# Cosformer attention into Sinkhorn-routed experts on one core: Sinkhorn's column total by an all-ones product, the second expert's weights in the load buffers, the last block's second layer in quarters, another order for the fourth batch

## The chip, the cores and the metric

The kernel runs on one core of one Trainium2 chip. The metric is device time in microseconds (us). Three runs of the kernel before gave 992.42, 992.71 and 993.43 us; the median is 992.71 us. A profiled execution, whose trace is used below, took 992.42 us, of which the hardware profiler's span is 990.7 us.

## What is computed

A linear attention over 8 batches of 8 heads, 576 positions and 64 features feeds a mixture of 8 experts, in which every token goes through every expert and the results are summed with weights from a Sinkhorn balancing. Cut to what matters:

```python
# attention: q, k, v are [8, 8, 576, 64]
phi(x) = concat(relu(x) * cos(pos), relu(x) * sin(pos))      # 128 features
num = phi(q) @ (phi(k).T @ v);   den = phi(q) @ phi(k).sum(over positions) + 1e-6
x = num / den, as [4608 tokens, 512]
# experts
P = exp(x @ w_gate - max)                                    # [4608, 8]
for _ in range(8):
    P /= P.sum(1) + 1e-9          # rows: each token over the experts
    P /= P.sum(0) + 1e-9          # columns: each expert over the tokens
    P *= 4608 / 8
out = sum over e of P[:, e] * (relu(x @ w1[e]) @ w2[e])      # w1: 512 x 1024, w2: 1024 x 512
```

## The kernel before

Tokens are kept transposed as matmul operands (`xT`, fp16), and results gather in fp32 accumulators (`acc_lo`, and `acc_hi` for the last four groups of 128 tokens). Parts of the accumulators that are not needed yet are lent to the attention: tables, two of the eight transposed-q buffers (`q_pTs`, numbers 6 and 7 in `acc_lo` and `acc_hi`) and the fp16 values.

The first phase mixes attention with the first expert. Block j of 512 tokens goes through that expert (8 `ffn1` slots of 4 matmuls, then 8 `ffn2` slots of 4 matmuls, so 16 slots) while batch j+1 gets its attention, and batch j+2's q, k and v are being loaded. Which step of the attention stands in which slot is written out by hand with `at(block, slot, step)`. The steps of a batch are, for each of its four head pairs hk:

- `load`: six DMAs of 288 KB, issued by POOL (GpSimd), one for each half of q, k and v, into the `ld` pool with four buffers of each. A load with `held_back` waits for the last VectorE (DVE) instruction that was written before it.
- `prep_q`: ReLU and the multiplication with the cosine and sine table on DVE, into one of three `q_p` buffers; from batch 2 on, the result is turned by a transposing DMA, issued by SP. The first of batch 3 also waits until that batch's last load has landed.
- `prep_k` (ReLU of k, on ScalarE, ACT), then `prep_kv`: `prep_kp` (the table's multiplication on DVE) and `prep_v` (a copy of v into its fp16 place).
- `sums`: the products of keys and values of two head pairs, whose results ACT and DVE bring to SBUF (`kv_sb`, `zsel`).
- `denominators`: 24 small matmuls over all transposed q of the batch, then DVE's reciprocal.
- `attend`, one for each hk: matmuls spread the reciprocals (`rb`, copied by ACT) and make the numerators; DVE multiplies the two into `xT`.
- `gates`: logits of a batch's tokens and their exponential.

TensorE, DVE and ACT run in the written order (`te`, `ve` and `se` chain each instruction to the one before it on its engine). SP and POOL are ordered by the framework's scheduler. So an instruction that waits holds all that is written behind it on its engine.

At the end of the first phase its pools are freed and other pools take the memory. The second expert's weights (`wB`, 16 KB in each partition) come first there, so they lie where the first pools of the phase lay: before, `hA` (the first expert's hidden values `hT`, in use until the last ffn2 of block 6), `cs_pool` (small constants) and part of `ld`.

Blocks 7 and 8 of the first expert follow with the Sinkhorn balancing (`sinkhorn`, a generator that yields five times in each of its 8 iterations, and that `balanced` moves on), then the first part of expert 1 with the seven-product method: each `group` calls a fill function seven times, and the first time round `start_fill` puts in a share of block 8's ffn2 and a step of the balancing. Some of those steps carry sums and differences of expert 1's first weights (`w1_steps`), dealt out to iterations by `tw_steps`. The remaining experts follow in a regular stream of products to the end.

In Sinkhorn, P lies as 128 partitions x 36 groups x 8 experts. A column total needs a sum over partitions: before, a matmul with a column of ones gives totals on one partition, DVE takes the reciprocal of these 8 numbers, and a second matmul with a row of the constant N/E spreads them to all partitions, where DVE multiplies.

Of the kernel before, what the change touches and what calls it, by code (L numbers as in the profile page):

```python
# [10 lines left out]
FP32 = mybir.dt.float32  # L11
# [14 lines left out]
def kernel(  # L26
# [154 lines left out]
    with ExitStack() as p1:  # L181
        hA = p1.enter_context(tc.tile_pool(name="hA", bufs=1))
        cs_pool = p1.enter_context(tc.tile_pool(name="cs_pool", bufs=1))
# [5 lines left out]
        rb_pool = p1.enter_context(tc.tile_pool(name="rb_pool", bufs=4))  # L189
        ps_y = p1.enter_context(tc.tile_pool(name="ps_y", bufs=2, space=bass.MemoryType.PSUM))  # L190
# [120 lines left out]
        scale_row = const.tile([1, 2, P], FP32, name="scale_row")  # L311
        ve.memset(scale_row[:, 0, :], float(N) / float(E))
        ve.memset(scale_row[:, 1, :], float(N) / float(E) / XS)
# [338 lines left out]
        for j in range(B):  # L652
            b = j + 1
            if j == 0:
# [4 lines left out]
                for hk in range(HK):  # L659
                    if hk == 3:  # L660
                        at(0, 7, sums_first, 0)
                    for i in range(3):
                        at(0, (5, 6, 6, 7)[hk], turn, 1, hk, i, i != 1)
                    if hk == 0:
                        at(0, 5, prep_q, 1, 3)
                    if hk >= 2:
                        at(0, 4 + hk, prep_v, 1, 2 * hk - 4, se.copy)
                        at(0, 4 + hk, prep_v, 1, 2 * hk - 3, ve.tensor_copy)
                at(0, 7, sums_first, 1)
# [4 lines left out]
            elif b < B:  # L674
# [14 lines left out]
                elif j == 2:  # L689
                    at(j, 0, prep_kv, b, 3)  # L690
                    at(j, 1, sums, b, 0)
                    at(j, 3, sums, b, 1)
                else:
                    at(j, 0, sums, b, 1)
                at(j, 6 if j == 1 else 5 if j == 2 else 3, denominators, b)
                for hk in range(HK):
                    at(j, (9, 10, 12, 13)[hk] if j == 1 else (8 if j == 2 else 6) + 2 * hk, attend, b, hk)
# [558 lines left out]
```

The softmax here doesn't subtract the row's maximum and nothing guards it: scores larger than these inputs give would overflow.

## Time and profile before

| | |
|---|---|
| median of three runs | 992.71 us |
| the profiled execution | 992.42 us |
| its span in the trace | 990.7 us |
| TensorE busy | 969.6 us, 98% |
| VectorE busy | 807.7 us, 82% |
| ScalarE busy | 564.1 us, 57% |
| GpSimd busy | 60.7 us, 6% |
| chain that ended last | TensorE 93%, DMA 2%, VectorE 2%, ScalarE 2% |

The busy share says how full an engine is on the average over the whole span. The list of waits says whom an engine waited for, and how long. A time line gives instructions in order of start, and a window sums them over a stretch. The granted clock is TensorE's share of its full clock. An idle engine costs nothing by itself; only what moves the last engine's end does.

### The profile page before, as it was taken

What the parts mean: (1) busy time and instruction counts of PE and PEld (TensorE: products, weight loads), DVE (VectorE), ACT (ScalarE), POOL (GpSimd) and SP (SyncE); (2) the same over time, 40 slices, a digit from 0 to 9 for tenths busy, and PEclk for the clock granted to TensorE, in tenths of its full rate; (3) what the DMA queues carried; (4) which work ended last, traced back from release to release, by engine and by line L of the source; (5) the groups of instructions that cost most, each with busy time, mean ns of one, the idle gap of its engine ahead of it and who ended that gap; (6) DMA issues with size and microseconds to landing.
All of it is one profiled execution on the core that took longest, in us unless ns stands there. A gap on an engine that the chain in (4) does not pass through costs nothing.

```text
span 990.7 us, 20271 instructions
## 1 busy us (share of the span) xinstructions
PE 969.6 (98%) x7871; PEld 675.4 (68%) x7871; DVE 807.7 (82%) x1835; ACT 564.1 (57%) x1261; POOL 60.7 (6%) x82
## 2 busy tenths in 40 slices
PE   9997999989999999999999999999999999999997
PEld 6443444447777777777777777777777777777775
DVE  7765675679889878988889888988789888988887
ACT  5763665457776555555555555555555555555551
POOL 6231110010000000000000000000000000000001
PEclk9997999999999999999999999999999999999999
DMA  9997991623013310043113410133103400104535
GB/s 162 181 150 113 161 153 33 133 46 88 26 49 68 63 53 25 25 91 67 33 41 67 82 34 25 43 74 68 49 25 67 92 24 26 48 25 111 133 85 128
DMA packets 80336, 73.54 MB, mean 74 GB/s; under 512 B 33264, under 2 KB 72176, under 8 KB 80240
## 3 DMA queue, kind: packets, MB, share of 16 engines
q0 software_dynamic: 27232, 30.94, 20.2%
q1 hardware_dynamic: 52768, 41.06, 16.9%
q8 instruction: 61, 1.00, 0.4%
q14 instruction: 35, 0.29, 0.1%
q10 hardware_dynamic: 240, 0.26, 0.1%
HBM read 83.12 MB, written 12.98 MB: 97 GB/s over the span
## 4 chain that ended last, share of the span: by engine, by line
PE 93%; DMA 2%; DVE 2%; ACT 2%; POOL 1%; issue 0%; POOLq 0%; ACTq 0%; SPq 0%
PE rows_ps L109 34%; PE h_ps L109 27%; PE copied_ps L109 11%; PE p_ps L109 11%; PE y_ps L109 6%; PE small_ps L109 4%; DMA acc_hi<-q_p 1%; DMA k_ld<-in_k_dram 1%; ACT hT L109 0%; DVE acc_hi L929 0%; POOL hs_last L944 0%; DVE P_tok L109 0%; DMA out_dram<-acc_lo 0%; DVE colp L109 0%; ACT u L109 0%
## 5 line engine op out<-in xcount | busy, mean ns | idle before, releaser
L929 DVE SCALAR_TENSOR_TENSOR acc_lo<-rows_ps,P_tok,acc_lo 128x512 f32<-128x512 f32 (+1 forms) x322 | 203.5, 641 | 74.5 <-PE rows_ps L109 74.4
L109 PEld LDWEIGHTS <-H 128*128 128x128 f16 x2080 | 203.0, 98 | 83.1 <-issue 1.2
L865 ACT CAST u<-h_ps 128x384 f16<-128x384 f32 x288 | 137.6, 478 | 131.3 <-PE h_ps L109 131.3
L109 PEld LDWEIGHTS <-w1e 128*128 128x128 f16 x1632 | 156.9, 98 | 67.3 <-issue 7.5
L859 DVE CUSTOM_DVE_ANT_0 H<-p_ps,u 128x384 f16<-128x384 f32 x329 | 181.4, 551 | 7.0 <-PE p_ps L109 6.3
L109 PEld LDWEIGHTS <-hs 128*128 128x128 f16 x1500 | 146.6, 98 | 56.2
L109 PE MATMUL h_ps<-S,w1e 128*128 128x384 f16 x672 | 164.1, 326 | 1.1 <-ACT u L109 0.9
L109 PE MATMUL p_ps<-xT,T 128*128 128x384 f16 x672 | 164.1, 326 | 0.1
L109 PE MATMUL h_ps<-xT,w1e 128*128 128x384 f16 (+1 forms) x616 | 151.5, 354 | 0.1
L109 PE MATMUL rows_ps<-V,H 128*128 128x256 f16 x1000 | 150.0, 273 | 0.7 <-DVE acc_hi L929 0.7
L109 PE MATMUL rows_ps<-w2e,hs 128*128 128x256 f16 x1000 | 150.0, 273 | 0.0
L897 ACT ACTIVATE H<-h_ps 128x384 f16<-128x384 f32 x144 | 70.6, 490 | 95.1 <-PE h_ps L109 95.1
L109 PEld LDWEIGHTS <-T 128*128 128x128 f16 x1008 | 98.1, 98 | 29.3 <-issue 2.8
L109 PE MATMUL rows_ps<-w2e,H 128*128 128x256 f16 (+1 forms) x568 | 91.2, 285 | 0.0
L878 ACT COPY copied_ps<-h_ps 128x384 f32<-128x384 f32 x144 | 67.5, 469 | 35.3 <-PE h_ps L109 35.3
L888 ACT ACTIVATE H<-copied_ps 128x384 f16<-128x384 f32 x144 | 70.8, 492 | 20.4 <-PE copied_ps L109 20.4
L109 PE MATMUL copied_ps<-xT,w1e 128*128 128x384 f16 x336 | 82.1, 326 | 0.0
L109 PE MATMUL h_ps<-S,T 128*128 128x384 f16 x336 | 81.8, 325 | 0.3 <-ACT copied_ps L109 0.3
L109 PE MATMUL copied_ps<-w2e,H 128*128 128x256 f16 x504 | 75.5, 272 | 0.0
L109 PE MATMUL rows_ps<-V,hs 128*128 128x256 f16 x500 | 75.0, 272 | 0.0
L929 DVE SCALAR_TENSOR_TENSOR acc_lo<-copied_ps,P_tok,acc_lo 128x256 f32<-128x256 f32 x126 | 60.2, 478 | 0.4
L929 DVE SCALAR_TENSOR_TENSOR acc_hi<-rows_ps,P_tok,acc_hi 128x512 f32<-128x512 f32 (+1 forms) x56 | 41.3, 738 | 19.9 <-PE rows_ps L109 19.1
(147 smaller groups left out, 952.5 us busy)
## 6 DMA issues: line engine op xcount, KB each, us to landing
S<-x_saved SPq DMA_DIRECT2D x108, 192.0 KB, 2.4
out_dram<-acc_lo SPq DMA_DIRECT2D x62, 128.0 KB, 2.4
w1e<-in_moe_w_dram POOLq DMA_DIRECT2D x7, 1024.0 KB, 9.1
w2e<-in_moe_w_dram POOLq DMA_DIRECT2D x7, 1024.0 KB, 9.7
q_ld<-in_q_dram POOLq DMA_DIRECT2D x16, 288.0 KB, 6.9
k_ld<-in_k_dram POOLq DMA_DIRECT2D x16, 288.0 KB, 8.3
v_ld<-in_v_dram POOLq DMA_DIRECT2D x16, 288.0 KB, 9.4
x_saved<-S SPq DMA_DIRECT2D x18, 192.0 KB, 1.9
```

Source lines behind the costliest of these rows:

```text
L109: i = getattr(self.engine, name)(*args, **kwargs)
L859: latest = ve._custom_dve(TENSOR_ADD_SAT, out=out, in0=ps[:, 0:TU], in1=t[:], s0=FP32_MAX, s1=0.0)
L865: se.copy(out=t[:], in_=ps[:, 0:TU])
L878: se.copy(out=Y[:, 0:TU], in_=X[:, 0:TU])
L888: se.activation(out=h11, in_=Y[:, 0:TU], func=AF.Relu)
L897: se.activation(out=h12, in_=X[:, 0:TU], func=AF.Relu)
L929: ve.scalar_tensor_tensor(out=a, in0=rows, scalar=P_tok[:, g, self.e : self.e + 1], in1=a, op0=ALU.mult, op1=ALU.add,)
```

## The change

It does five things.

1. The pools of the first phase are opened in another order: `hA` and `cs_pool` last instead of first. The second expert's weights thus lie on the load buffers alone.
2. Sinkhorn's column total is one matmul with a 128 x 128 matrix of ones, which leaves the total on every partition. DVE takes the reciprocal on all partitions, and one `scalar_tensor_tensor` multiplies P by it and by the constant. The second matmul and its constant rows are gone. The weight sums of expert 1 stand in iterations 1 to 4 instead of 3 to 6.
3. Block 8's ffn2 is dealt out in quarters (2 matmuls), at fills 0, 2, 3 and 5 of each seven, instead of halves (4 matmuls) at fills 0 and 3.
4. Block 1 prepares batch 3's keys and values one or two slots earlier, and completely: the last head pair's `prep_kp` and `prep_v` (on ACT) stand in slot 14, and `sums(3, 0)` in slot 15. Block 2 is then written like the later blocks: `sums(3, 1)` in slot 0, `denominators` in slot 3 instead of 5, `attend` from slot 6 instead of 8, the preparation of batch 4 one slot earlier, batch 5's loads in slots 11 and 12 instead of 12 and 13.
5. In block 0 the copies of batch 1's values go to ACT and DVE in another order, and both `sums` stand after the last turn of q.

```diff
     with ExitStack() as p1:
-        hA = p1.enter_context(tc.tile_pool(name="hA", bufs=1))
-        cs_pool = p1.enter_context(tc.tile_pool(name="cs_pool", bufs=1))
         ld = p1.enter_context(tc.tile_pool(name="ld", bufs=4))
...
         rb_pool = p1.enter_context(tc.tile_pool(name="rb_pool", bufs=4))
+        cs_pool = p1.enter_context(tc.tile_pool(name="cs_pool", bufs=1))
+        hA = p1.enter_context(tc.tile_pool(name="hA", bufs=1))
...
-        scale_row = const.tile([1, 2, P], FP32, name="scale_row")
...
+        ones_all = const.tile([P, P], FP32, name="ones_all")
+        ve.memset(ones_all[:], 1.0)
...
                 for hk in range(HK):
-                    if hk == 3:
-                        at(0, 7, sums_first, 0)
                     for i in range(3):
                         at(0, (5, 6, 6, 7)[hk], turn, 1, hk, i, i != 1)
                     if hk == 0:
                         at(0, 5, prep_q, 1, 3)
-                    if hk >= 2:
-                        at(0, 4 + hk, prep_v, 1, 2 * hk - 4, se.copy)
-                        at(0, 4 + hk, prep_v, 1, 2 * hk - 3, ve.tensor_copy)
-                at(0, 7, sums_first, 1)
+                    if hk == 2:
+                        at(0, 6, prep_v, 1, 0, se.copy)
+                        at(0, 6, prep_v, 1, 2, ve.tensor_copy)
+                    if hk == 3:
+                        at(0, 7, prep_v, 1, 1, se.copy)
+                        at(0, 7, prep_v, 1, 3, ve.tensor_copy)
+                for half in range(2):
+                    at(0, 7, sums_first, half)
...
-                elif j == 2:
-                    at(j, 0, prep_kv, b, 3)
-                    at(j, 1, sums, b, 0)
-                    at(j, 3, sums, b, 1)
                 else:
                     at(j, 0, sums, b, 1)
-                at(j, 6 if j == 1 else 5 if j == 2 else 3, denominators, b)
+                at(j, 6 if j == 1 else 3, denominators, b)
                 for hk in range(HK):
-                    at(j, (9, 10, 12, 13)[hk] if j == 1 else (8 if j == 2 else 6) + 2 * hk, attend, b, hk)
+                    at(j, (9, 10, 12, 13)[hk] if j == 1 else 6 + 2 * hk, attend, b, hk)
...
                 for slot, fn, hk in (
-                    (4, prep_q, 0), (5, prep_q, 1), (8, prep_q, 2), (10, prep_k, 0),
-                    (11, prep_k, 1), (11, prep_kv, 0), (12, prep_q, 3), (12, prep_k, 2),
-                    (13, prep_kv, 1), (13, prep_k, 3), (15, prep_kv, 2),
+                    (4, prep_q, 0), (5, prep_q, 1), (8, prep_k, 0), (8, prep_q, 2),
+                    (9, prep_k, 1), (10, prep_kv, 0), (10, prep_k, 2), (12, prep_q, 3),
+                    (12, prep_kv, 1), (12, prep_k, 3), (13, prep_kv, 2), (14, prep_kp, 3),
+                    (14, prep_v, 3),
                 ) if j == 1 else (
-                    (5, prep_q, 0), (6, prep_k, 0), (6, prep_q, 1), (7, prep_k, 1),
-                    (8, prep_q, 2), (9, prep_kv, 0), (9, prep_k, 2), (10, prep_q, 3),
-                    (11, prep_k, 3), (11, prep_kv, 1), (13, prep_kv, 2), (14, prep_kv, 3),
+                    (4, prep_q, 0), (5, prep_k, 0), (5, prep_q, 1), (6, prep_k, 1),
+                    (7, prep_q, 2), (8, prep_kv, 0), (8, prep_k, 2), (9, prep_q, 3),
+                    (10, prep_k, 3), (10, prep_kv, 1), (12, prep_kv, 2), (13, prep_kv, 3),
                 ) if j == 2 else (
...
-                    at(j, slot, fn, b + 1, hk)
-                if j > 1:
-                    at(j, 15 if j == 2 else 14, sums, b + 1, 0)
+                    at(j, slot, fn, b + 1, hk, *((se.copy,) if fn is prep_v else ()))
+                at(j, 15 if j == 1 else 14, sums, b + 1, 0)
             if j == 1:
                 for name in "qkv":
                     for half in range(2):
                         at(j, 12, load, b + 2, half, name, True)
             elif j and b + 2 < B:
                 for half in range(2):
-                    at(j, 11 + (j == 2) + half, load, b + 2, half, "qkv", True)
+                    at(j, 11 + half, load, b + 2, half, "qkv", True)
...
-            tot_ps = small[0][0:1, :]
-            te.matmul(out=tot_ps, lhsT=ones_col[:], rhs=colp[:], start=True, stop=True)
-            t2 = sk_pool.tile([1, E], FP32, name="t2")
-            ve.reciprocal(out=t2[:], in_=tot_ps)
+            te.matmul(out=total, lhsT=ones_all[:], rhs=colp[:], start=True, stop=True)
             for step in tw_steps[it][2:]:
                 step()
             yield
-            te.matmul(
-                out=small[1], lhsT=scale_row[0:1, 1 if it == 7 else 0, :], rhs=t2[0:1, :],
-                start=True, stop=True,
-            )
-            ve.tensor_tensor(
+            t2 = sk_pool.tile([P, E], FP32, name="t2")
+            ve.reciprocal(out=t2[:], in_=total)
+            ve.scalar_tensor_tensor(
                 out=P_tok[:], in0=P_tok[:],
-                in1=small[1].unsqueeze(1).to_broadcast([P, NG, E]), op=ALU.mult,
+                scalar=float(N) / float(E) / (XS if it == 7 else 1.0),
+                in1=t2[:].unsqueeze(1).to_broadcast([P, NG, E]),
+                op0=ALU.mult, op1=ALU.mult,
             )
             yield
...
-        tw, tw_steps[3 + i] = w1_steps(w_next, i)
+        tw, tw_steps[1 + i] = w1_steps(w_next, i)
...
-        tiles = halves(hT, w0, [(ts * P, j * TCH // P + ts) for ts in range(TCH // P)])
+        tiles = dealt(
+            hT, w0, [(ts * P, j * TCH // P + ts) for ts in range(TCH // P)],
+            2 if j < NJ - 1 else 4,
+        )
...
-        if k_fill % 7 in (0, 3):
+        if k_fill % 7 in (0, 2, 3, 5):
             next(tiles, None)
```

`dealt` is `halves` with the number of parts as an argument.

More of the change, by code (lines that the diff above doesn't have):

```diff
@@ L310 @@
         ve.memset(ones_col[:], 1.0)
-        scale_row = const.tile([1, 2, P], FP32, name="scale_row")
-        ve.memset(scale_row[:, 0, :], float(N) / float(E))
-        ve.memset(scale_row[:, 1, :], float(N) / float(E) / XS)
+        ones_all = const.tile([P, P], FP32, name="ones_all")
+        ve.memset(ones_all[:], 1.0)
         eps_row = cs_pool.tile([1, 32], FP32, name="eps_row")
@@ L1025, in sinkhorn @@
     def sinkhorn():
-        small = (W2[:, 0:E], W2[:, TCH - E : TCH])
+        total = W2[:, 0:E]
         for it in range(8):
@@ L1065, in balanced, with dealt @@
             next(balance, None)
-    def halves(hT, w, tiles):
+    def dealt(hT, w, tiles, parts):
         for i, (c0, g) in enumerate(tiles):
-            for part in range(2):
+            for part in range(parts):
                 ffn2(
                     hT, w, c0, g, rows2[i % 3][:],
-                    range(part * FT // 2, (part + 1) * FT // 2),
+                    range(part * FT // parts, (part + 1) * FT // parts),
                 )
```

## The prediction

> **What bounds the kernel now.** I read the page's busy line first, then TensorE's waits, then the windows and time lines around each wait. The profiled execution took 992.42 us (span 990.7 us), 0.3 us below the median of 992.71 us; sums are made on 992.42.
>
> ```profile
> PE 969.6 (98%) x7871; PEld 675.4 (68%) x7871; DVE 807.7 (82%) x1835; ACT 564.1 (57%) x1261; POOL 60.7 (6%) x82
> ```
>
> TensorE's waits (engine, tile, line, what it waited for: us, times, longest):
>
> ```profile
> PE small_ps L109 <- DMA acc_hi<-q_p: 8.4, 1, 8.4
> PE copied_ps L109 <- DVE colp L109: 2.0, 2, 1.2
> ```
>
> TensorE is busy 98%, so only its gaps and its own work can move the time. Of its 21 us of gaps, one wait of 8.4 us stands alone; next comes Sinkhorn's column total with 2.0 us.
>
> ```profile
> 65.50:73.10 7.60, 7.60 (x116) 3.85 (x114) 4.53 (x13) 4.98 (x11) 4.31 (x6) 1.00 1.13 152
> 73.10:81.50 8.40, 0.03 (x3) 0.00 (x0) 0.00 (x0) 0.05 (x1) 0.00 (x0) 0.77 1.22 173
> 81.50:87.80 6.30, 6.25 (x36) 2.62 (x36) 4.33 (x8) 2.53 (x5) 0.00 (x0) 0.50 0.18 35
> 200.00:222.00 22.00, 19.11 (x105) 9.36 (x103) 16.85 (x45) 12.73 (x27) 4.37 (x4) 1.00 0.29 50
> ```
>
> The windows (stretch, sum, then PE, PEld, DVE, ACT, POOL, granted clock, DMA share, GB/s) show every engine empty from 73.1 to 81.5 us while the DMA engines are full, and the clock at 0.50 until 87.8 us. The stall so costs 8.4 us and (87.8 - 81.5)/2 = 3.1 us more: 11.5 us. From 200 to 222 us TensorE is idle 2.9 us.
>
> ```profile
> 64.09 1.29 SPq L362 DMA_TRANSPOSE q_pT<-q_p  x1
> 65.49 1.33 SPq L362 DMA_TRANSPOSE acc_lo<-q_p  x1
> 66.99 2.09 SPq L362 DMA_TRANSPOSE acc_hi<-q_p  x1
> ```
>
> ```profile
> 65.86 1.43 POOL L202 DMA_DIRECT2D q_ld<-in_q_dram  x2 [10.26 <-DVE q_p L109]
> 67.28 1.45 POOL L202 DMA_DIRECT2D k_ld<-in_k_dram  x2
> 68.70 1.47 POOL L202 DMA_DIRECT2D v_ld<-in_v_dram  x2
> ```
>
> These are SP's and POOL's time lines: the last transpose of batch 3 (counting from 0, the "fourth batch") is issued at 66.99 us, the six loads of batch 4 from 65.86 us, released by the DVE instruction that makes that same q_p. The transpose lands after 14.5 us, where the median is 3.4.
>
> [...] Counting packets by half microseconds, two transposes alone run at about 780 packets/us; the loads' first packets come at 68.3 us, just as the third transpose (1,152 packets) would begin, and it then gets about 15/us for 2 us and 140/us after, so it ends with the loads. [...]
>
> **The change by parts.**
>
> (a) *Batch 1's values in block 0.* The same copies in another order. Before, the first sums wait 0.34 us and the second 1.14 us for ACT's value copies. After, ACT has one copy more ahead of the first sums: they run at 33.2 to 34.6 us instead of ending at 34.76. Taken: -0.15 (bounds -0.5, +0.5).
>
> (b) *Batch 3's keys and values two slots earlier.* ACT meets the first key ReLU in slot 8, at 56.6 us, but those keys land at 52.73 + 6.0 = 58.8 us. Queued behind it on ACT are one acc copy (0.5) and two rb copies (0.6).
>
> ```profile
> 55.96 0.60 ACT L109 ACTIVATE hT<-h_ps 128x512 f16<-128x512 f32 x1 [1.14 <-PE h_ps L109]
> 57.69 0.58 ACT L109 COPY acc_lo<-y_ps 128x512 f32<-128x512 f32 x1 [1.13 <-PE y_ps L109]
> 58.17 0.71 ACT L109 COPY rb<-small_ps 128x384 f32<-128x384 f32 x2
> ```
>
> With the ReLU's 0.6, the rb copies end at 60.5 instead of 58.8, and xT follows on DVE. TensorE wants these PSUM buffers for the next attend at 59.1: it waits to 60.4, and 0.3 more for xT. Taken: +1.5 (bounds 0.8, 2.5). Then sums(3,0) and sums(3,1), 0.7 us each, precede slots 15 and 1; the last key product on DVE is ready about 68.9, so +0.25.
>
> (c) *Denominators of batch 3 in slot 3 instead of 5.* TensorE comes there two ffn1 groups earlier (2 x 4 matmuls, 0.86 us each: 1.73). Its arrival was 72.45; now 72.45 + 1.5 + 0.25 - 1.73 - 0.15 = 72.3, and 73.0 at the head pair that needs the last transpose. Those 1.73 us now lie behind it.
>
> (d) *What the loads wait for.* They are still written in slot 12, after DVE's last instruction there. That was the fourth q_p (ends 65.5); now one key product (0.67) and one value copy (0.37) follow it. POOL so issues about 1.05 us later, and the first load packets come near 69.3 instead of 68.3. The fourth q_p itself waits for an earlier transpose that lands at 64.7, and SP is not free before 66.9, so the transpose stays at 66.99; its packets start near 68.35. Until they are starved (about 0.3 us after the loads' first) there are 1.25 us x 780 = 975 of 1,152; the rest needs 2 us at 15 and about 1.1 us at 140. It lands near 73.4 with the 0.5 us that the landing took after the last packets. TensorE resumes at 73.4 instead of 81.55: -8.15, +1.73 for the work moved behind, and the clock is not dropped, -3.1. Sum -9.5. With batch 4's keys landing near 76.5, ACT's ReLU in slot 5 is held half a microsecond and DVE's fourth q_p somewhat; I allow +0.5. Taken: **-9.0**. This is the term with the widest bounds: -10.7 with no wait at all and no hold, and above nothing in the rivals.
>
> (e) *Block 2's other steps* (attend, preparation, loads of batch 5, sums(4,0)) move up by one or two slots together: the same instructions, and batch 5's loads keep their distance of two slots from the last transpose, as in blocks 3 to 5, where TensorE has no wait. Zero; the cover is that distance, and without it a stall like block 2's would follow.
>
> (f) *Memory order.* The second expert's weights no longer overlap hT, which frees only at 175 us, but the load buffers, whose last readers are block 5's. POOL's two issues (1.7 us together) move from 177.1 to about 154 us. The DMA share from 155 to 175 us is 0.01, and block 5's transposes are all but out by then. Weights land before 175 instead of 186.8 and 193. No TensorE wait names them, so zero by itself (bounds 0, +1); it is what lets the weight sums move to iterations 1 to 4.
>
> (g) *Sinkhorn.* Per iteration, gone: a total on one partition, whose pair of fp32 instructions takes 0.12 us to the next start (180.84 to 180.96), and a broadcast pair with 128 weight columns, 0.32 us (181.93 to 182.25). New: one pair with 128 weight columns, not in the trace; nearest row, the broadcast, 0.32 (bounds 0.12 and 0.44, since row count may matter). Saved 8 x 0.12 = 1.0 us (0 to 2.6). On DVE the reciprocal (0.19) and the product (0.45) stay; an fp32 scalar_tensor_tensor of 288 elements is bounded by that product and by 0.48, the row for 256 elements from PSUM. DVE's two waits per iteration become one, so the product can start one fill earlier, and iterations 5 and 6 lose four weight sums (about 0.9 us of DVE each); iterations 1 and 2, where DVE sits idle 1.9 and 0.9 us, take them. The two colp waits (1.20 and 0.78 us) should shrink by about two thirds: -1.3. Taken: **-2.3** (bounds +0.5, -4).
>
> (h) *Quarters.* The same 32 matmuls for the last block, spread over four fills in seven instead of two. No instruction more. It spaces ACT's u copies (0.9 us of waits in three places); its gain is inside (g)'s bound, as is the loss if a tile's evacuation comes two fills later.
>
> Sum: -0.15 - 9.0 - 2.3 = -11.4 (b and c are inside d): 992.4 - 11.4 = **981.0**, 981.3 against the median.
>
> **The rivals.**
>
> *The transpose still lands in the loads (partly).* If the loads' packets come only 0.5 us later, about 500 packets are left, and it lands at 77 to 80. [...] For: one microsecond decides, between two queues. Against: DVE's two instructions surely precede the loads. d is then -4 to +1, the total 986 to 992.
>
> *Slower: the loads win as before.* Place: the same wait. If the transpose is cut off from its first packets, it ends with the loads, which are 1.0 to 1.7 us later (b delays DVE too): resume at 82.5 to 83.2, +1.0 to +1.7, plus 1.73 of work behind it, less 0.4 of clock: +2.3 to +3.0, with Sinkhorn at -2.3 to 0: 992.4 to 995.4. It decides where the transpose lands after 82 us, the break-even with (g). For: a transpose issued at 54.54 among loads took until 64.7. Against: there the loads were ahead.
>
> *The change does not do what it says in Sinkhorn*: the chain is hidden, or TensorE waits for the same DVE work in another place. g is 0 and the total 983.3. For: DVE is 77% busy from 200 to 222. Against: two waits carry its name.
>
> **Numbers.** Chances: forecast, with or without (g), 0.65 (978.5 to 985.5); partly 0.15 (985.5 to 992); loads win 0.15 (992 to 995.5); anything else, mainly an ACT hold larger than in (b), 0.05. About 0.2% (2 us) is what a measurement of this kernel can tell from no change: faster, below 990.7, is 0.65 + 0.11 = 0.76; same 0.11; slower 0.13. The range 978.5 to 992.5 leaves 0.2 out.
>
> **What would show it.** Right: the wait on acc_hi<-q_p under 2 us, clock 1.00 throughout the middle, a new TensorE wait of about 1.5 us near 60 us for ACT's rb, colp waits under 1 us together, expert 1's weights issued near 154 us. Wrong: the transpose landing above 77 us, or the clock at 0.5 after it.

## The result and the profile after

Four runs of the kernel after gave 980.48, 981.09, 981.16 and 981.30 us, median **981.12 us**. The kernel before, beside them, had a median of 992.57 us. The ratio is **0.9883** (95% interval 0.9866 to 0.9900): 1.2% faster. The prediction was 981.3 us. The profiled execution took 980.48 us, its span 978.8 us. The sum was right; its largest term was met partly by luck, as the last sections show.

The page of the kernel after (busy us, share of the span, instructions; then the granted clock in 40 slices):

```profile
PE 964.4 (99%) x7855; PEld 674.2 (69%) x7855; DVE 807.1 (82%) x1833; ACT 565.2 (58%) x1262; POOL 60.6 (6%) x82
PEclk9999999999999999999999999999999999999999
```

TensorE's waits in the kernel after:

```profile
PE copied_ps L109 <- DVE colp L109: 3.0, 4, 1.2
PE small_ps L109 <- DMA acc_hi<-q_p: 0.8, 1, 0.8
PE small_ps L109 <- ACT acc_lo L109: 0.7, 1, 0.7
PE small_ps L109 <- ACT rb L109: 0.5, 1, 0.5
```

The wait of 8.4 us for the last transpose of batch 3 is down to 0.8 us, and no slice shows a lower clock. But the wait for Sinkhorn's `colp` did not shrink by two thirds: it grew from 2.0 to 3.0 us. To see where the 11.9 us of span came from, cut both traces at the same instructions: the first gates product of batches 1, 2, 3 and 7, and the first two products of the weight and x sums (`copied_ps<-xT`) of expert 1, which the expectations below call the first and the second Sinkhorn mark. A stage is what lies between two of these instructions. Windows of the kernel before, then of the kernel after (stretch, length, then PE, PEld, DVE, ACT, POOL, granted clock, DMA share, GB/s):

```profile
52.65:81.99 29.34, 20.91 (x236) 10.25 (x232) 14.12 (x33) 13.46 (x32) 7.26 (x11) 0.92 1.07 153
81.99:104.22 22.23, 22.23 (x207) 10.39 (x205) 15.83 (x34) 13.11 (x30) 4.31 (x6) 0.87 0.67 112
...
175.93:199.11 23.18, 23.02 (x129) 10.36 (x128) 16.89 (x40) 10.26 (x18) 1.66 (x2) 1.00 0.70 134
199.11:220.71 21.60, 18.97 (x105) 9.36 (x104) 16.44 (x44) 12.27 (x26) 4.51 (x4) 1.00 0.29 50
```

```profile
51.97:74.74 22.77, 21.40 (x238) 10.46 (x234) 15.46 (x34) 13.44 (x32) 7.21 (x11) 1.00 1.05 158
74.74:94.28 19.54, 19.54 (x206) 9.62 (x205) 14.12 (x33) 13.61 (x31) 4.28 (x6) 1.00 1.12 177
...
165.98:187.44 21.46, 21.42 (x122) 10.23 (x121) 17.49 (x45) 10.27 (x18) 0.00 (x0) 1.00 0.12 45
187.44:208.64 21.20, 17.88 (x96) 9.05 (x95) 16.15 (x39) 12.06 (x25) 4.17 (x4) 1.00 0.30 53
```

- Start of the first two windows: block 0 is done at 51.97 us instead of 52.65: **-0.68**.
- 52.65 to 104.22 took 51.57 us before; the same work takes 42.31 after: **-9.26**. The first window loses TensorE's idle time (8.43 to 1.37), the second the stretch at half clock (22.23 to 19.54).
- 175.93 to 220.71 (Sinkhorn) took 44.78 us, after 42.66: **-2.12**. TensorE's busy time falls by 2.69 us (41.99 to 39.30), and its idle time rises by 0.57 (2.79 to 3.36).
- The rest, to the end of the span, took 770.00 us before and 770.14 us after.

How the transpose and the loads met, in SP's and POOL's time lines of the kernel after:

```profile
64.62 1.30 SPq L361 DMA_TRANSPOSE acc_lo<-q_p  x1
66.10 1.46 SPq L361 DMA_TRANSPOSE acc_hi<-q_p  x1
```

```profile
66.01 1.43 POOL L202 DMA_DIRECT2D q_ld<-in_q_dram  x2 [11.10 <-DVE acc_lo L109]
67.43 1.43 POOL L202 DMA_DIRECT2D k_ld<-in_k_dram  x2
```

The loads are now released by the value copy (`DVE acc_lo`) instead of by the fourth `q_p`, and are issued 0.09 us ahead of the last transpose instead of 1.13 us. The transpose lands at 72.68 us, 6.6 us after its issue instead of 14.5. Counted in half microseconds, though, its packets did not get the head start that the prediction gave them:

| from (us), kernel after | 67.0 | 67.5 | 68.0 | 68.5 | 69.0 | 69.5 | 70.0 | 70.5 | 71.0 | 71.5 | 72.0 |
|---|---|---|---|---|---|---|---|---|---|---|---|
| packets of the loads | 1 | 19 | 19 | 47 | 55 | 51 | 64 | 13 | 3 | 61 | 94 |
| packets of the transposes | 264 | 6 | 19 | 50 | 56 | 46 | 104 | 361 | 297 | 237 | 8 |

The loads' first packets come at 67.5 us, just as the last packets of the transpose in progress go out, and the last transpose gets almost nothing at first (6 packets against 19), then about as many as the loads (50 against 47, 56 against 55, 46 against 51). Some 280 of its 1,152 are out by 70.5 us. The rest leaves in 1.5 us, around a pause of the loads between their first 256 packets and the second load. In the kernel before there was no such pause.

### The profile page after: what moved, and what is told of

Same layout as the page of the kernel before. It is cut to its first block, busy times and chain, and to the rows that moved or that the text cites. A ratio compares the mean times of both kernels' runs of the same rounds, so it can differ in the third digit from the quotient of the medians.

```text
span 978.8 us, 20237 instructions
## 1 busy us (share of the span) xinstructions
PE 964.4 (99%) x7855; PEld 674.2 (69%) x7855; DVE 807.1 (82%) x1833; ACT 565.2 (58%) x1262; POOL 60.6 (6%) x82
## 4 chain that ended last, share of the span: by engine, by line
PE 88%; DMA 4%; DVE 3%; issue 2%; ACT 1%; POOL 1%; POOLq 0%; ACTq 0%; SPq 0%
PE rows_ps L109 33%; PE h_ps L109 26%; PE p_ps L109 11%; PE copied_ps L109 11%; PE y_ps L109 4%; PE small_ps L109 3%; DMA k_ld<-in_k_dram 1%; DMA w2e<-in_moe_w_dram 1%; DMA w1e<-in_moe_w_dram 1%; DMA acc_hi<-q_p 1%; DVE P_tok L109 1%; DVE colp L109 0%; POOL q_ld L202 0%; DVE rs L109 0%; DVE acc_hi L926 0%
## 5 line engine op out<-in xcount | busy, mean ns | idle before, releaser
L109 PE MATMUL h_ps<-xT,w1e 128*128 128x384 f16 (+1 forms) x616 | 149.4, 350 | 0.1
L875 ACT COPY copied_ps<-h_ps 128x384 f32<-128x384 f32 x144 | 67.5, 469 | 35.1 <-PE h_ps L109 35.1
L109 PE MATMUL copied_ps<-w2e,H 128*128 128x256 f16 x504 | 75.5, 272 | 0.0
```

The lines of the kernel that those rows point to most:

```text
L109: i = getattr(self.engine, name)(*args, **kwargs)
L875: se.copy(out=Y[:, 0:TU], in_=X[:, 0:TU])
```

## The experiments

**Theory T.** Two causes: the order of the loads and the last transpose (about 9 us, clock included) and the second product of each Sinkhorn iteration (about 2 us). The pool order, the weight sums' place and the quarters are worth nothing by themselves. **Rivals:** the saving comes from block 2's new order (work moved behind the wait) rather than from the loads; the Sinkhorn saving belongs to the edits around it; a head start of either side decides nothing, only a pause does. The ratios below are to the kernel before; where parts are compared, the stages of the traces, cut as above, carry more than the run medians, which scatter by 1 to 7 us.

### The new order of blocks 1 and 2 alone (before, with part 4 of the change)

```diff
-                    (4, prep_q, 0), (5, prep_q, 1), (8, prep_q, 2), (10, prep_k, 0),
+                    (4, prep_q, 0), (5, prep_q, 1), (8, prep_k, 0), (8, prep_q, 2),
...
-                at(j, 6 if j == 1 else 5 if j == 2 else 3, denominators, b)
+                at(j, 6 if j == 1 else 3, denominators, b)
...
```

> The kernel before with the new order of blocks 1 and 2 alone (batch 3's keys and values, denominators, attend, batch 4's preparation). Theory 1, head start: the loads come after most of the transpose's packets, so the wait on acc_hi<-q_p is under 1.5 us, the clock stays at 1.00, and the total falls by about 9.3 us to 983.3. Theory 2, the pause: the transpose is starved from its first packets and only ends early where the loads pause between the first and the second; the same total if that pause recurs, else a wait of 5 us or more and a total of 988 to 993. Rival 3: another part of the change helped (block 0's order gave 0.7 us), then the total stays above 985.

Measured: 984.18 us, ratio 0.9935 (0.9914 to 0.9956). The stage from the gates of batch 1 to those of batch 7 took 114.82 us (before 123.28, after 114.01): -8.46. The wait for the transpose was 0.7 us, the clock was not lowered. So in this trace the part carries nearly all of the stage's saving by itself. Of the two pictures expected here the packets say the second: the last transpose got 27 to 77 packets in half a microsecond beside the loads, and 887 of its 1,152 left around a pause of theirs of 0.63 us. The median hides two clusters: three runs took 983.5 to 984.2 us, two 987.4 and 987.6. In these two the mean granted clock was 0.998, in the others 0.999 to 1.000, as if the wait had come back in part; no trace of them was kept.

### The old order, loads one slot later (before, slot 13)

```diff
-                        at(j, 12, load, b + 2, half, name, True)
+                        at(j, 13, load, b + 2, half, name, True)
```

> The kernel before with one change: batch 4's six loads are written in slot 13 of block 1 instead of slot 12, so POOL issues them about 1.7 us later (67.6 instead of 65.9). Theory 1: about 1,150 packets of the last transpose go first; it lands near 71, the wait of 8.4 us and the half clock go, the total is 981 to 982.5 (11.5 us less, perhaps 0.5 to 1 us of it given back where batch 4's keys land later). Theory 2: loads issued within about 1 us of the transpose starve it again; it lands after 75 us, and the total stays above 985.

Measured: 982.86 us, ratio 0.9907 (0.9887 to 0.9926); the same stage took 114.19 us. Nothing of the schedule was moved but the six loads, and it saves 9.1 us. The loads are issued 0.57 us behind the transpose, whose packets now all but finish first: 404 in the half microsecond from 69.5, 42 in the next, when the loads begin. It lands at 72.39, and TensorE does not wait for it. The later loads have a price of their own: ACT waits 2.45 us for batch 4's keys, and TensorE then for ACT:

```profile
PE y_ps L109 <- ACT hT L109: 1.2, 1, 1.2
```

The landing is later than the expected 71 us, and the median 0.4 us above the expected range (981 to 982.5). The rival that the moved work makes the saving falls.

### After, with the loads released by the fourth q_p again

```diff
                     at(j, slot, fn, b + 1, hk, *((se.copy,) if fn is prep_v else ()))
+                    if j == 1 and fn is prep_q and hk == 3:
+                        for name in "qkv":
+                            for half in range(2):
+                                at(j, 12, load, b + 2, half, name, True)
...
-            if j == 1:
-                for name in "qkv":
-                    for half in range(2):
-                        at(j, 12, load, b + 2, half, name, True)
...
```

> The changed kernel with one change: batch 4's loads are written in slot 12 straight after the fourth q_p, ahead of the key product and value copy, so that POOL issues them about 1.05 us earlier against the transpose, as in the kernel before. Theory 1: the transpose ends with the loads, at about 80 us; the wait is back at 7 to 9 us with the half clock after it; the total is 990 to 993. Theory 2: it is starved as in the changed kernel and ends in the pause between the first two loads; wait under 3 us, total 981 to 983.

Measured: 990.86 us, ratio 0.9985 (0.9979 to 0.9992), ten microseconds given back by one release. TensorE's wait, and windows of this kernel (the wait; the stretch at half clock):

```profile
PE small_ps L109 <- DMA acc_hi<-q_p: 8.8, 1, 8.8
```

```profile
71.90:80.80 8.90, 0.18 (x9) 0.03 (x1) 0.00 (x0) 0.21 (x1) 0.00 (x0) 0.70 1.20 171
75.50:85.70 10.20, 4.84 (x32) 2.05 (x32) 4.11 (x8) 1.36 (x4) 0.00 (x0) 0.50 0.56 92
```

The wait and the clock's drop are back, with all other edits in place. The stage took 124.41 us.

### After, with the loads in between

They are released by the key product of the second head pair, one DVE instruction ahead of the kernel after.

```diff
-                    (12, prep_kv, 1), (12, prep_k, 3), (13, prep_kv, 2), (14, prep_kp, 3),
+                    (12, prep_kp, 1), (12, prep_k, 3), (13, prep_kv, 2), (14, prep_kp, 3),
...
+                    if j == 1 and fn is prep_kp and hk == 1:
+                        for name in "qkv":
+                            for half in range(2):
+                                at(j, 12, load, b + 2, half, name, True)
+                        at(j, 12, prep_v, b + 1, 1, ve.tensor_copy)
...
```

> The kernel after with batch 4's loads released one DVE instruction earlier (between the key product and the value copy of the second head pair), so that they are issued 0.4 to 0.5 us ahead of the last transpose instead of 0.1 us ahead. Theory (what counts is whose packets are ready when the transpose in progress ends; the pause between the first and the second load then lets the last one out): as in after the loads get in first, the pause between them is shorter because the first load has had longer to be followed by the second; the transpose lands at 73.5 to 77 us, TensorE waits 1.5 to 5 us[...]: 1 to 7 us over after. Rival (the pause is of fixed length and always comes): within 0.5 us of after. Rival (any head start is enough for the loads): as with loads 1.2 us ahead, a wait of 8 us or more and 9 to 10 us over after.

Measured: 989.19 us, ratio 0.9971 (0.9959 to 0.9982). SP's and POOL's time lines and the wait of this kernel:

```profile
66.82 1.53 SPq L361 DMA_TRANSPOSE acc_hi<-q_p  x1
```

```profile
66.38 1.43 POOL L202 DMA_DIRECT2D q_ld<-in_q_dram  x2 [11.42 <-DVE k_p L109]
```

```profile
PE small_ps L109 <- DMA acc_hi<-q_p: 6.4, 1, 6.4
```

The loads are 0.44 us ahead, no pause follows their first 256 packets, and the transpose lands at 79.00: later than the theory gave (77 at most), and with a shorter wait than the second rival's 8 us or more. The rival of a pause that always comes falls. One thing is unlike the kernel before: there the loads caught the tail of the transpose ahead, which landed only at 71.61 us; here that one was out when the loads came (landed at 68.65), so the last one went out beside them from 69 us on. 0.35 us of lead separate this kernel from the kernel after, and 8.9 us of time in the stage.

### After, with the loads in slot 13

```diff
-                        at(j, 12, load, b + 2, half, name, True)
+                        at(j, 13, load, b + 2, half, name, True)
```

> The kernel after with batch 4's loads written in slot 13 of block 1 instead of slot 12, so that they are issued about 1 us behind the last transpose's issue instead of 0.1 us ahead of it. Theory[...]: the transpose's packets all go first, it lands near 70.5 us, 1.5 us ahead of TensorE, and the wait of 0.8 us on acc_hi<-q_p is gone; the loads come 1 to 2 us later and may hold ACT's key ReLU by some tenths: the time is 0.3 to 0.8 us under the kernel after, 980.3 to 980.8. Rival (later loads are paid back in full by ACT and DVE of block 2): as after or up to 1 us over it. Rival (DVE, not the transpose, is the last to be ready there): the wait only changes its name and the time stays within 0.2 us.

Measured: 981.20 us, ratio 0.9894 (0.9880 to 0.9908). The transpose lands at 69.98, 3.5 us after its issue, close to the median of 3.4 us of the transposes in the kernel after, and its wait is gone. But this execution waited 1.0 us instead of 0.5 us for `rb` near 60 us, which is before the loads are issued. The stage took 114.01 us, to the hundredth that of the kernel after, and the runs (980.2 to 982.9) lie around those of the kernel after. The theory's 0.3 to 0.8 us is not seen; whether the 0.8 us of wait is a gain can't be told.

### What all the traces say of this meeting

Each line is one profiled execution. "Lead" is the loads' issue minus the last transpose's issue.

| kernel | lead, us | loads' first packet after their issue | pause after the first 256 | transpose lands after its issue | TensorE's wait |
|---|---|---|---|---|---|
| after, released by q_p | -1.19 | 2.58 | none | 14.5 | 8.8 |
| before, all-ones product | -1.16 | 2.47 | none | 14.4 | 8.3 |
| before | -1.13 | 2.47 | none | 14.5 | 8.4 |
| after, in between | -0.44 | 1.86 | none | 12.2 | 6.4 |
| before, new order | -0.11 | 1.52 | 0.63 | 6.4 | 0.7 |
| after, three edits undone | -0.10 | 1.51 | 0.51 | 7.2 | 1.4 |
| after | -0.09 | 1.49 | 0.52 | 6.6 | 0.8 |
| after, early weight sums | -0.07 | 1.48 | 0.51 | 6.9 | 1.1 |
| after, totals twice | +0.20 | 2.74 | none | 6.5 | 0.4 |
| after, old block 0 | +0.25 | 2.48 | none | 5.8 | none |
| before, slot 13 | +0.57 | 2.15 | none | 5.0 | none |
| after, slot 13 | +1.64 | 1.42 | none | 3.5 | none |
| after, both small moves | +2.01 | 1.42 | none | 3.2 | none |

Undisturbed, the loads' first packet comes 1.42 us after their issue (batches 6 and 7 of the kernels before and after). Where it was later, it came as the packets of a transpose ran out. With leads of -0.44 to -0.07 us all 1,152 packets of the transpose in progress are out by then. With the three leads near -1.15 us, 96 to 178 of them are still to come; with leads of +0.20 to +0.57 us, 6 to 145 of the last transpose's own. In the eight traces with a negative lead the loads went next, ahead of the transpose that had not begun. So in these traces the last transpose was either ahead of the loads but for 145 packets at most (positive leads) or behind their start (negative ones), and in the second case the pause decided.

Where the loads caught the tail of a transpose, that tail was slow. In the kernel before, the transpose ahead of the last one landed 6.1 us after its issue, at 71.61 us; in the kernel after it takes 3.3. SP's time line, and the landing from the view of its tile:

```profile
65.49 1.33 SPq L362 DMA_TRANSPOSE acc_lo<-q_p  x1
DMA to landing us min/median/max: 6.1/6.1/6.1
```

Of the 113 transpose packets between the loads' first one and that landing, 96 were its own and 17 the last transpose's, whose other packets then went out beside the loads for 9.6 us. Why the tail went so slowly, some 30 packets/us, is not shown.

### The all-ones product alone (before, with it)

```diff
-            te.matmul(out=tot_ps, lhsT=ones_col[:], rhs=colp[:], start=True, stop=True)
+            te.matmul(out=total, lhsT=ones_all[:], rhs=colp[:], start=True, stop=True)
...
-            te.matmul(
-                out=small[1], lhsT=scale_row[0:1, 1 if it == 7 else 0, :], rhs=t2[0:1, :],
...
```

> The kernel before with Sinkhorn's all-ones total alone (weight sums, memory order and halves as before). The prediction's step: 8 x 0.12 = 1.0 us less on TensorE and the two colp waits (2.0 us) shrinking by up to two thirds, total 990.3. Theory from the trace after: the pair of matmuls costs less than the one it replaces and a break in the stream is saved, about 0.3 us in each iteration (2.4 us), while the colp waits stay at 2 us or more; total 990 to 990.5 with colp waits of 2 to 3 us. If the chain is hidden: 992.5.

Measured: 990.01 us, ratio 0.9983 (0.9976 to 0.9991). The Sinkhorn stage took 42.69 us (before 44.78, after 42.66): -2.09, the whole of the stage's saving, although the `colp` waits rose here too:

```profile
PE copied_ps L109 <- DVE colp L109: 2.8, 4, 1.6
```

### After, each total computed twice

```diff
             te.matmul(out=total, lhsT=ones_all[:], rhs=colp[:], start=True, stop=True)
+            te.matmul(out=total, lhsT=ones_all[:], rhs=colp[:], start=True, stop=True)
```

> The kernel after with each of the eight all-ones products of Sinkhorn issued twice in a row (the second writes the same numbers over the first). Theory (each fp32 pair that stands between two streams of TensorE costs its full time to the next start, 0.14 to 0.25 us, whatever DVE does, and this is where the 2.1 us came from): 8 x 0.14 to 0.25 = 1.1 to 2.0 us over the kernel after, all of it between the start of the last block and the second Sinkhorn mark, and colp waits within 0.5 us of 3.0. Rival (TensorE has slack there, and DVE's chain sets the pace): under 0.4 us over after, with colp waits smaller by what the second products cost. Rival (the price is the break of the stream, paid once for both): 0.3 to 0.8 us.

Measured: 981.82 us, ratio 0.9900 (0.9885 to 0.9915), which does not stand clear of the kernel after (the medians are 0.7 us apart, the spans 1.3); the Sinkhorn stage of the trace took 43.76 us, +1.10. Its `colp` wait:

```profile
PE copied_ps L109 <- DVE colp L109: 2.5, 3, 1.0
```

An fp32 product stands in the trace as a pair of instructions. The second pair adds 0.22 us in each iteration: about 0.36 us to the next start where one pair takes 0.14, 0.47 where one takes 0.24. That is 1.8 us over the eight, of which the stage shows 1.10; the rest, 0.5 us of it for `colp`, went into waits that were there anyway. By the stage the cost is at the low end of what the theory gave and over the rivals' 0.4 and 0.8; the run medians alone would not exclude the latter. So a pair of fp32 products on this stretch has a price of its own. The second stands behind the first rather than behind another stream, so it need not be the price of the one that was removed.

### After, with the weight sums in iterations 0, 1, 2 and 2

```diff
-        tw, tw_steps[1 + i] = w1_steps(w_next, i)
+        tw, steps = w1_steps(w_next, i)
+        tw_steps[(0, 1, 2, 2)[i]] += steps
```

> The kernel after with the four weight sums of the second expert in Sinkhorn's iterations 0, 1, 2 and 2 instead of 1 to 4. Theory (DVE's chain sets the end of the column totals where weight sums and x sums lie in one iteration): the longest of the four waits on colp (1.2 us, near 190 us) shrinks to under 0.4 us, colp waits fall from 3.0 to about 2 us, and the time by 0.8 to 1 us, to about 980.2. Rival (TensorE only meets the same DVE work elsewhere, DVE being the engine with no slack from 180 to 200 us): colp waits of 2.5 to 3.5 us in other iterations and no difference over 0.3 us.

Measured: 980.76 us, ratio 0.9883 (0.9871 to 0.9896). The `colp` waits were 2.7 us, the longest 0.9; the Sinkhorn stage took 42.30 us, -0.36. The longest wait did not fall under 0.4 us: most of it moved to other iterations, as the rival said. The stage fell by slightly more than the rival's 0.3 us, and took 42.30 us again in the last experiment; the runs don't tell it from nothing.

### After, with pool order, weight sums and halves as before

```diff
+        hA = p1.enter_context(tc.tile_pool(name="hA", bufs=1))
+        cs_pool = p1.enter_context(tc.tile_pool(name="cs_pool", bufs=1))
...
-        cs_pool = p1.enter_context(tc.tile_pool(name="cs_pool", bufs=1))
-        hA = p1.enter_context(tc.tile_pool(name="hA", bufs=1))
...
-        tw, tw_steps[1 + i] = w1_steps(w_next, i)
+        tw, tw_steps[3 + i] = w1_steps(w_next, i)
...
-            2 if j < NJ - 1 else 4,
+            2,
...
-        if k_fill % 7 in (0, 2, 3, 5):
+        if k_fill % 7 in (0, 3):
```

> The kernel after with three of its edits undone together: the old order of the SBUF pools, weight sums in iterations 3 to 6, and the last block's second layer in halves. Theory (the prediction's e to h: none of the three has a worth of its own): within 0.5 us of after, expert 1's weights issued near 166 us, colp waits 2.5 to 3.5 us, the stage from the last block's start to the second Sinkhorn mark within 0.4 us of the kernel after. Rival (they carry part of the saving in the last block): 1 to 2 us slower, with colp or ACT waits larger by that much.

Measured: 981.56 us, ratio 0.9893 (0.9880 to 0.9906). Expert 1's weights were issued at 167.87 us, the Sinkhorn stage took 43.05 us (+0.39), and the waits for `u` rose from 0.6 to 1.3 us while `colp` stood at 2.8. Between this and the all-ones product alone (42.69), the three edits are worth 0 to 0.4 us together, perhaps the quarters' shorter waits for `u` (with halves and the all-ones product alone they are 1.2 us). Each by itself was not tried.

### After, with block 0 as before

```diff
-                for half in range(2):
-                    at(0, 7, sums_first, half)
+                at(0, 7, sums_first, 1)
```

(and the value copies in their old order)

> The kernel after with batch 1's value copies and first sums of block 0 as before. The kernel after reaches the gates of block 1 at 51.97 us, the kernel before at 52.65 us: 0.68 us, where 0.15 was predicted. Theory (the reordered copies are worth the predicted 0.15, the rest is how early the first loads land in one execution or another): the time is 0.1 to 0.3 us over after. Rival (the whole 0.68 us belongs to the reorder): 0.6 to 0.7 us over after, with TensorE waits for ACT's value copies near 34 us of 0.7 us or more in sum.

Measured: 982.18 us, ratio 0.9905 (0.9887 to 0.9923), the gates of batch 1 at 52.63 us: +0.66. TensorE's wait in this kernel:

```profile
PE small_ps L109 <- ACT acc_lo L109: 1.5, 2, 1.1
```

That is the line of the kernel before; the kernel after has 0.7 us in one wait. The five traces with the old block 0 have these gates between 52.30 and 52.78, the eight with the new one between 51.63 and 52.30, and the means are 52.62 and 51.97: the reorder is worth about 0.65 us. The traces so speak for the rival. The run median is 1.1 us over the kernel after, but its runs lie between 980.5 and 987.9 us; the longest had a mean granted clock of 0.998, and no trace of it was kept.

### Both small moves (slot 13, early weight sums)

```diff
-                        at(j, 12, load, b + 2, half, name, True)
+                        at(j, 13, load, b + 2, half, name, True)
...
+        tw_steps[(0, 1, 2, 2)[i]] += steps
```

> The kernel after with both small moves together: batch 4's loads in slot 13 and the weight sums in iterations 0, 1, 2 and 2. Each alone took 0.24 and 0.36 us out of its own stage of the trace, less than the runs tell apart. Theory (they lie in different stages and add): 0.5 to 0.9 us under after, no wait on acc_hi<-q_p, colp waits 2.7 us. Rival (each is within what one execution differs from the next, and the ReLU of batch 3's first keys decides as much by itself): within 0.4 us of after.

Measured: 980.21 us, ratio 0.9879 (0.9866 to 0.9893): faster than the kernel before by 1.2%, and not to be told apart from the kernel after. The transpose landed 3.2 us after its issue; the `rb` wait near 60 us was 1.1 us. By the ratios it is 0.4 us under the kernel after, by the spans of the traces 0.1 us over it. The theory's 0.5 to 0.9 us is not shown, and the rival not excluded.

## Why the prediction was right, and where it was not

**(a) Block 0: -0.15 predicted, -0.68 measured.** A mis-sized term. The step counted that the first sums would run a little earlier. TensorE's waits there, 1.5 us for ACT's `acc_lo`, became 0.7 us for it and 0.3 us for DVE's `acc_hi`. The step put all 72 products of both sums behind ACT's last copy, at 33.2 to 34.6 us. That copy came when it said, but a quarter of the products had run by then, and the others were done at 34.10 instead of 34.76. TensorE in the kernel after:

```profile
31.95 0.44 PE L109 MATMUL small_ps<-acc_lo,k_p 64*128 64x65 f16 x17 [0.35 <-DVE acc_hi L109]
33.13 1.03 PE L109 MATMUL small_ps<-acc_lo,k_p 64*128 64x65 f16 x54 [0.74 <-ACT acc_lo L109]
34.10 1.04 PE L109 MATMUL y_ps<-w2e,hT 128*128 128x512 f16 x4
```

The result lies outside the step's bound of -0.5.

**(b) ACT's hold near 60 us: +1.5 predicted, 0.5 measured** (up to 1.4 us in the other traces with the new order). The mechanism is there: ACT waited 1.61 us for the keys. But they landed 5.5 us after their issue instead of 6.0, and TensorE met only the last part. A hold by a DMA's landing should carry the landing's scatter.

**(c), (d) The transpose: -9.0 predicted, -9.27 measured from the gates of batch 1 to those of batch 7.** The cause is shown: releasing the loads by `q_p` again brings the wait and the half clock back (8.8 us, 124.41 us for the stage). The relative shift of the two issues was right as well (1.05 predicted, 1.04 measured). The picture of what follows was wrong, and that the number was met is partly luck. The step let the first load packets come 2.4 us after their issue, as in the trace before, which would have let 975 packets go first. Those 2.4 us held a wait for the transpose in progress; undisturbed they are 1.42 us. So in both kernels the loads were there before the last transpose had begun, at 68.3 us before and 67.5 after, and it was cut off from its first packets. That was the trigger of the rival "the loads win as before". (The step also read the 15 packets/us after 68.3 us as the last transpose's; most were the tail of the one ahead of it, and all but 17 of its own came from 71.6 us on.) That the transpose did not end with the loads in the kernel after is due to the pause of the loads at 70.5 us, which no step foresaw. With 0.44 us of lead the rival's mechanism is what happens, with 6.4 us of wait instead of 8.4, since the transpose ahead was out in time. The 1.73 us of work that (c) put behind the wait had no worth of its own: with the old order and later loads there was no wait for the transpose, and the stage was as short (114.19 us). The chance given to the partial and the losing cases together, 0.30, was not too high: the kernel after stands 0.35 us of lead from one of them, and two of the five runs with the new order alone were 3.8 and 4.0 us longer than its profiled one.

**(e) and (f): zero, and zero measured.** From the gates of batch 3 to those of batch 7 the time is 71.7 us in both. Expert 1's weights were issued at 147.3, not near 154 us; nothing waited for them in either case.

**(g), (h) Sinkhorn: -2.3 predicted, -2.12 measured, by two errors that cancel.** TensorE's time lines, of the kernel before and of the kernel after:

```profile
180.84 0.20 PE L109 MATMUL copied_ps<-colp,ones_col 128*1 128x8 f32 x2
180.96 1.04 PE L109 MATMUL h_ps<-xT,w1e 128*128 128x512 f16 x4
181.93 0.38 PE L109 MATMUL copied_ps<-t,scale_row 1*128 1x8 f32 x2
182.25 0.61 PE L109 MATMUL h_ps<-xT,w1e 128*128 128x512 f16 x2
```

```profile
179.27 0.59 PE L109 MATMUL rows_ps<-w2e,H 128*128 128x512 f16 x2
179.90 0.39 PE L109 MATMUL copied_ps<-colp,ones_all 128*128 128x8 f32 x2
180.15 0.59 PE L109 MATMUL h_ps<-xT,w1e 128*128 128x512 f16 x2
```

```profile
170.80 0.28 PE L109 MATMUL copied_ps<-colp,ones_all 128*128 128x8 f32 x2
170.94 1.89 PE L109 MATMUL h_ps<-xT,w1e 128*128 128x512 f16 x8
172.66 2.75 PE L109 MATMUL rows_ps<-w2e,H 128*128 128x512 f16 x12
```

To the next start the old products took 0.12 and 0.32 us. The new one takes 0.14 us in the two iterations whose sums were ready in time (170.80 to 170.94) and 0.24 to 0.25 us in the six others, where the step took 0.32. The step also left out what stands ahead of a product. Four long products take 0.86 us in a full stream (eight in 1.72 us, 170.94 to 172.66), but 0.97 us ahead of the second old product (180.96 to 181.93): each old product held the stream up by 0.1 us more, the new one, when its sums are ready, by nothing. The two old ones so cost 0.65 us, not 0.44, and without the waits 0.4 to 0.5 us of it was saved in each iteration, where the step had 0.12. TensorE's busy time, as the profile counts it, fell by 2.7 us over the eight. Against it the `colp` waits, which were to shrink by 1.3 us, grew by 1.0. The reading that fits is that TensorE, freed from the second product, comes to the same DVE chain sooner: four iterations out of eight now wait instead of two. The experiment that took only this edit shows both halves again (-2.09 us in the stage, TensorE's busy time 3.0 us less, 2.8 us of `colp` waits).

The sum on the span: -0.68 - 9.27 - 2.12 + 0.14 = -11.93 us; the profiled runs differ by 992.42 - 980.48 = 11.94 us.

**What stays open.** Why the loads pause in the four traces with a lead of -0.07 to -0.11 us and in none of the others was not settled. One candidate, DVE's work in fp16 in the 2 us after the loads' issue, was the same with and without a pause (1.83 us in the kernels before and after), so that alone does not make it. The transpose's issue on SP takes 1.27 us undisturbed, 1.46 in the kernel after and 2.09 in the kernel before; in the kernel before one at 129.59 us takes 2.08, 3 us after the last packet of any load, so the loads alone do not explain it.

## What to carry to other kernels

Where two queues feed a transfer that the critical engine waits for, look at which of them is ready when the transfer in progress ends, not only at the issue times: here one DVE instruction more or less ahead of a bulk load moved its stage by 8.9 us, and a one-word change (slot 13) got most of the gain without the new schedule. Put a bulk load clearly behind the small transfer that is due next, by a dependency and not by a fraction of a microsecond. And when a product is taken off an engine that waits for another, cost the engine's own time and the wait apart. The first falls by all that the product breaks off the stream, ahead of it too (0.65 us here, not 0.44); the second can grow, as the engine comes early (3.0 us instead of 2.0).

## What the runs showed of the hardware that was not expected

- Once both were under way, the loads and the transpose sent about equal numbers of packets in the kernel after: 50 against 47, 56 against 55, 46 against 51 in half a microsecond. With no load beside them the transposes sent some 800/us (416, 393, 422 and 386 in half a microsecond from 65.5 us on in the kernel before); beside the loads the last transpose sent 92 to 112/us in the kernel after, and 118/us over 9.6 us in the kernel before, which is what made it land so late there. The prediction had counted some 15/us for it at first. In the kernel after only the first half microsecond is so uneven (19 against 6); the longer uneven stretch of the kernel before, 330 against 80 packets from 68.5 to 71.5 us, is the tail of the transpose ahead.
- In these traces a transpose that had begun went all but to its end first: the loads' first packets came up to 2.74 us after their issue, against 1.42 us undisturbed, when none to 178 of its 1,152 packets were left. A tail that was caught was slow: with 96 to 178 left, the transpose landed some 6 us after its issue instead of 3.3.
- From 60 to 90 us the mean granted clock was 1.00 in the nine traces with a wait of at most 1.4 us for the transpose, and lower in the four with a long one. In the kernel before it was 0.50 from 77.6 to 87.8 us: the drop came 4.5 us after TensorE fell idle, and ended 6.3 us after it resumed; half of that, 3.1 us, is the estimate of its cost. In the kernel after with the loads released by `q_p` it was 0.50 from 75.5 to 85.7 us, from 3.6 us after TensorE fell idle. The mean from 60 to 90 us was 0.83 with waits of 6.4, 8.4 and 8.8 us, and 0.89 with 8.3 us in the kernel with the all-ones product alone. By an estimate from these means, TensorE had half clock for 10.2 us in the first three and for 6.6 us in that one, after much the same stall as in the kernel before. The spans of these two (990.7 and 987.0 us) differ by 3.7 us, of which 2.1 are Sinkhorn's; the other 1.6 fit the shorter half clock. The twenty runs of that kernel differ in the same way: 988.0 to 989.4 us with a mean granted clock of 0.996, 991.6 to 992.7 us with 0.993, the others between.
- A pair of fp32 instructions with 128 x 128 weights and 8 columns took 0.14 us to the next start in a full stream of the kernel after (170.80 to 170.94 us) and held up nothing ahead of it, less than the pair with one row of weights that it replaced (0.32 us, and 0.1 us ahead of it), although it has 128 times the weights. Where its sums came late it took 0.24 to 0.25 us.
